# A decode-step gradient kernel: w1's gradient pass run backwards, its space lent slot by slot, a fifth wq chunk kept, and three zero-fill pieces moved

## The chip, the cores and the metric

The kernel runs on one core of one Trainium2 chip. The metric is the device time of one execution in microseconds; the median of several runs is compared. The core has a matrix engine (PE, whose weight loads are listed as PEld), a vector engine (DVE), an activation engine (ACT), a general engine (POOL), a queue engine that issues most DMAs (SP), and 16 DMA engines that move data between HBM and the on-chip memory.

## The reference

One token goes through two attention layers and two MLP layers that share their weights, and the result is the output and the gradients of all inputs but one.

```
x = x + A(layernorm(x)); x = x + B(layernorm(x))      # layer 0
x = x + A(layernorm(x)); x = x + B(layernorm(x))      # layer 1
A: q = n @ wq (1024 x 4096, 32 heads of 128); the last 4096 rows of a 32768-row cache, 4 kv heads;
   softmax(q k / sqrt(128)) v; @ wo (4096 x 1024)
B: h = n @ w1 + b1 (1024 x 3584); h * tanh(softplus(h)); @ w2 (3584 x 1024)
out = x, and by vjp(grad_out): gradients of x, k_cache, v_cache, wq, wo, w1, b1, w2
```

All is bf16. The gradients of the two caches are full size (32768 rows per head), and all rows but the last 4096 are zero. So a large part of the output is zeros, 56 pieces of 1 MB.

## The kernel before

The weights are too large to stay on the chip together, so they are read several times in chunks of 1 MB (128 partitions by 4096 bf16): wq and wo have eight chunks, w2 has seven, and w1 has eight parts of 896 KB, one for each t, which lie together in the tile W1 (W in the profile). The work stands in this order: forward through layers A, B, A, B; then the gradients backward, through B of layer 1 (dn_b1), A of layer 1 (attn_bwd with l = 1), B of layer 0 (the second reading of w2, then dn_b0), and A of layer 0 (attn_bwd with l = 0); then the outer products that make the weight gradients, and their stores. No planner reorders it: the order on each engine is the order in which the program is written, and waits between engines are put in from what each instruction reads and writes.

**The ring.** A class Ring holds eight slots of 1 MB. Loads are asked for with want, in a fixed order, and pump (L51 to L71) issues the next one on SP as soon as a slot is free. release frees the slot of a chunk when its last product has been written; keep renames a chunk in its slot, so that it needn't be loaded again; lend (L86) adds slots. Since SP issues DMAs in program order, whatever SP has to wait for holds up every load behind it.

**The chunks kept.** In attn_bwd of layer 1, the loop over wq's eight chunks (L915) transposes each chunk in place on PE in groups of eight blocks (L452), and DVE or ACT copies each group back (L305, L308). Chunks named in KEEP_Q2 (L268) stay in their slots, transposed, until attn_bwd of layer 0 uses them. The others are loaded again and transposed again.

**The second reading of w2** (L1102 to L1108). For each chunk c: mlp_out (L697), 32 products that finish the forward output; flush, which writes the products of the chunk before (L471); rows_chunk, two rows by DVE dot products (L429) and two by transposing; then the release of the chunk, which comes into effect after the next chunk's L697. Meanwhile the ring loads the rest of w2 and then wo (the key "o", 3).

**dn_b0** (L837). For each of the eight parts t of w1: a DVE dot over 512 columns and 24 products on PE. Behind parts 2 and 4 it writes row copies of vectors (rowize, take_back, rowize_f) into the space of w1's parts 0 and 1, ROWS and rf. They are small DMAs on SP: rowize first transposes on PE and copies on ACT (L978, L981), take_back reads back from DRAM what was put there. After dn_b0, lend gives the ring three more slots at once (L1118). They lie over w1's parts 4 to 7 (lent[0] over 4 and 5, lent[1] over 5 and 6, lent[2] over 6 and 7).

**attn_bwd of layer 0.** First the pass over wo's eight chunks with the hook do1(c) after each (rowize of GA at c = 0, and so on), then the scores' gradients with the hook dp1, then dq1, then the pass over wq with the hook dn1(t). The work units of the weight gradients (unit_dw, L1019, and units_kv, L1070) read ROWS and fill the rest of the time; they begin in dp1.

**The zero pieces.** zeros(n, after) (L256) issues n zero pieces from the tile zt on POOL's queue. With after, a tiny copy (L259) first waits until that value has been written; POOL works in order, so the pieces go out behind it. zt is set to zero in last_da (L761), which runs in the second attention's forward part, after the products with wq and before the scores. Until then zt holds a chunk of w2.

Of the kernel before, what the change touches and what calls it, by code (L numbers as in the profile page):

```python
# [23 lines left out]
TD = D // P  # L24
# [69 lines left out]
def kernel(  # L94
# [36 lines left out]
    def sb(shape, dtype, name):  # L131
        return keep.tile(shape, dtype, name=name)
# [3 lines left out]
    def tmp(shape, dtype, name):  # L136

        if name not in scratch:
            scratch[name] = keep.tile(shape, dtype, name=name)
        return scratch[name]  # L140
# [30 lines left out]
    def big():  # L171
        if wide:
            wide.append(wide.pop(0))
            return wide[-1][:, 0:512]
        b = bigs[big_n[0] % len(bigs)]
        big_n[0] += 1
        return b
# [22 lines left out]
    NA = sb([P, TD, 2], BF16, "NA")  # L200
    NB = sb([P, TD, 2], BF16, "NB")
    GA = sb([P, TD, 2], BF16, "GA")
    GB = sb([P, TD, 2], BF16, "GB")
    OC = sb([P, HQ, 2], BF16, "OC")
    DQC = sb([P, HQ, 2], BF16, "DQC")
    AC = sb([P, TF, 2], BF16, "AC")
# [13 lines left out]
    ring = Ring(nc, [ring_t[:, i, :] for i in range(8)])  # L220
# [9 lines left out]
    def want_q(k, ts=range(8)):  # L230
        for t in ts:
            ring.want(("q", k, t), wq_v[:, t, :], [P, J])

    def want_o(k, cs=range(8), homes=()):
        for c in cs:
            own = homes[c].rearrange("p (k d) -> p k d", k=4) if c < len(homes) else None
            ring.want(("o", k, c), wo_v[:, c], [P, 4, D], own, [("K", c)] if own is not None else [])
# [18 lines left out]
    def zeros(n, after=None):  # L256

        if after is not None and zjobs:
            nc.gpsimd.tensor_copy(pz[0:1, pz_n[0] % 16:pz_n[0] % 16 + 1], after[0:1, 0:1])  # L259
            pz_n[0] += 1  # L260
        for _ in range(n):
            if zjobs:
                dst = zjobs.pop()
                nc.gpsimd.dma_start(dst, zt[:])  # L264


    KEEP_Q = (5, 6, 7)
    KEEP_Q2 = (4, 5, 6, 7)  # L268
    EARLY_2 = (0, 1)
    MID_2 = (2, 3)  # L270
    W1S = W1[:].rearrange("p t f -> p (t f)")
# [17 lines left out]
    want_o(3)  # L289
    want_q(3, [t for t in range(8) if t not in KEEP_Q2])  # L290
    ring.pump()
# [35 lines left out]
    def bcast(col_of, n, dst=None):  # L327


        for i in range(n):  # L330
            k = i % 8
            nc.tensor.transpose(LB[i // 8][:, k * P:(k + 1) * P], col_of(i).to_broadcast([P, P]), ident_bf[:])
        if dst is not None:
            nc.vector.tensor_copy(dst, LB[0][:, 0:n * P])
# [87 lines left out]
    def rowdot(w, vecs, n, acc, fours=False):  # L422

        for i, vec in enumerate(vecs):
            out, a = junk[:, 0:n], w[:, i * n:(i + 1) * n]
            if fours:
                out, vec = (x.rearrange("a (k p) -> a k p", p=P) for x in (out, vec))
                a = a.rearrange("a (p k) -> a k p", k=4)
            nc.vector.tensor_tensor_reduce(out=out, in0=a, in1=vec, scale=1.0,  # L429
                                           scalar=acc if i else 0.0, op0=ALU.mult, op1=ALU.add, accum_out=acc)  # L430
        load["D"] += len(vecs) * (n * 1.1e-3 + 0.18)
# [33 lines left out]
    def mv_open():  # L465

        fresh[0] = True

    def mv(w, n, out, rhs_of, last):
        for i in range(n):  # L470
            nc.tensor.matmul(out, lhsT=w[:, i * P:(i + 1) * P], rhs=rhs_of(i), start=fresh[0], stop=last and i == n - 1,  # L471
                             skip_group_check=True)
            fresh[0] = False
# [3 lines left out]
    def turn_ahead(key, tts):  # L477

        for tt in tts:
            ahead[key, tt] = turn_pe(ring.get(key)[:, tt, :], TD)  # L480
# [152 lines left out]
    def conv(n, eng=None):  # L633
        for _ in range(n):
            conv_ev(conv_pe(1), eng)
# [92 lines left out]
    def da_dots(c, tts=range(4)):  # L728
        for tt in tts:
            r = 4 * c + tt  # L730
            rowdot(ring.get(("2", 0, c))[:, tt, :], [gbc], D, da1[:, r:r + 1])
# [21 lines left out]
    def last_da(k):  # L753

        for c in (5, 6):
            if k == 0:
                da_dots(c)
            else:
                ring.release(("2", 0, c))
        if k:  # L760
            nc.gpsimd.memset(zt[:], 0.0)  # L761

    def wo_hook1(c):
        if c == 0:
            zeros(7, OC[:, 0, 1:2])
        if c:
            conv(1)
# [13 lines left out]
    def take_back(name, base, off):  # L781
        r = DR[name][:].rearrange("(n l) p -> l n p", l=2)
        nc.sync.dma_start(ROWS[base:base + 2, off:off + r.shape[1] * P].rearrange("l (n p) -> l n p", p=P), r)
# [13 lines left out]
    dnp = sb([P, TD], FP32, "dnp")  # L797
# [18 lines left out]
    def rowize_f():  # L816

        b = big().bitcast(BF16)
        for l in range(2):
            for k in range(4):  # L820
                nc.tensor.transpose(b[0:7, (4 * l + k) * P:(4 * l + k + 1) * P],
                                    DHC[:, :, l].rearrange("p (c k) -> p k c", k=4)[:, k], ident_bf[:])
        nc.scalar.copy(rf.rearrange("c (l p k) -> c l p k", l=2, k=4), b[0:7].rearrange("c (l k p) -> c l p k", l=2, k=4))
        for l in range(2):
            nc.sync.dma_start(ROWS[64 + l:65 + l, NOFF:NOFF + F].rearrange("o (c j) -> o c j", j=512),
                              rf[:, 512 * l:512 * l + 512])
# [10 lines left out]
    def dn_b0(g):  # L837
        bcast(lambda c: DHC[:, c, 0:1], STAY)
        mv_open()
        for t in range(TD):  # L840
            rowdot(W1[:, t, 0:STAY * P], [LB[0][:, 0:512]], 512, dnp[:, t:t + 1], True)
            mv(W1[:, t, STAY * P:], TF - STAY, TP[:, t:t + 1], lambda i: DHC[:, STAY + i, 0:1], True)
            if t == 2:
                rowize(GB, TD, 96, 0)
                take_back("AC", 96, NOFF)
                take_back("NB", 64, 0)
                take_back("OC", 32, NOFF)
                take_back("NA", 0, 0)
            if t == 4:
                rowize_f()  # L850
        return ln_bwd(dnp, sB0["n32"], sB0["rstd"], g, "B0", lambda k: turn_ahead(("o", 3, 0), ((0,), (1, 2))[k]))

    DENSE = 2
# [100 lines left out]
    def dq3():  # L954
        zeros(3, DQC[:, 0, 1:2])

    g2 = attn_bwd(1, sA1, g3, ("o", 1), ("q", 2), KEEP_Q2,
                  dict(do=lambda c: conv(2 if 1 < c < 6 else 1), dp=dp3, dq=dq3, dn=lambda t: None),
# [4 lines left out]
    NOFF = 1024  # L963
# [7 lines left out]
    lent = [W1S[:, 16384 + i * SLOT:16384 + (i + 1) * SLOT] for i in range(3)]  # L971
# [3 lines left out]
    def rowize(cols, n, base, off):  # L975

        b = big().bitcast(BF16)
        nc.tensor.transpose(b[0:2 * n, 0:P], cols[:].rearrange("p n l -> p (n l)"), ident_bf[:])  # L978
        k = rt_n[0]
        rt_n[0] += 1  # L980
        nc.scalar.copy(rt[0:2 * n, k, :], b[0:2 * n, 0:P])  # L981
        for l in range(2):
            nc.sync.dma_start(ROWS[base + l:base + l + 1, off:off + n * P].rearrange("o (t p) -> o t p", p=P),
                              rt[l:2 * n:2, k, :])
# [40 lines left out]
    def units_rows(base, nblk, out):  # L1025

        for c in range(nblk // 4):
            s = stage_free.popleft()
            for tt in range(4):
                n = 0  # L1030
                while n < 2:
                    m = unit_dw(base, NOFF + (4 * c + tt) * P, 512 * n, s[:, tt * D + n * 512:(tt + 1) * D], 2 - n)
                    n += m
                    store(out.rearrange("(c p k) d -> p c (k d)", p=P, k=4)[:, c], s, 2 * tt + n - m, 2 * tt + n, 8,
                          c == nblk // 4 - 1)
                    yield
# [78 lines left out]
    nc.vector.tensor_copy(DHC[:, :, 0], dh0[:])  # L1115
    zeros(2, dh0)
    g1 = dn_b0(g2)
    ring.lend(lent)  # L1118
    nc.vector.tensor_copy(GA[:, :, 0], g1[:])

    x4 = sb([P, TD], BF16, "x4")
# [7 lines left out]
    do1_acc = tmp([P, HQ], FP32, "da")  # L1129

    def do1(c):
        if c == 0:
            rowize(GA, TD, 32, 0)
        if c == 3:
            todo[1].append(units_rows(32, HQ, out_5))
        if c == 5:
            store_rows(x4[:], TD, out_0[0, 0, :])
            store_f(db)
        if c == 5:
            zeros(2, do1_acc[:, 4 * c:4 * c + 1])  # L1140
# [10 lines left out]

    def dn1(t):
        if t in (3, 6, 7):
            zeros(2 if t == 3 else 1, dnp[:, t:t + 1])
        if t == 4:
            twins()
        if t == 5:
            todo[0].append(units_cols(0, 8, out_4))

    def units_a0(k):  # L1160
# [3 lines left out]
        work(4)  # L1164

    g0 = attn_bwd(0, sA0, g1, ("o", 3), ("q", 3), (), dict(do=do1, dp=dp1, dq=dq1, dn=dn1), units_a0)
    zeros(3, g0)
    g0b = sb([P, TD], BF16, "g0b")
    nc.vector.tensor_copy(g0b[:], g0[:])
    store_rows(g0b[:], TD, out_1[0, 0, :])  # L1170
# [46 lines left out]
```

## Time and profile before

| what | value |
|---|---|
| runs | 455.77 us median of 3 (455.38 to 458.13) |
| the profiled execution | 456.82 us, its span 455.0 us |
| busy in the span | PE 326.4, PE weight loads 262.1, DVE 258.8, ACT 210.6, POOL 38.8 us |
| moved by DMA | 181.48 MB, mean 399 GB/s |
| issued by SP or ACT / by POOL | 121.84 MB / 58.72 MB |

The page cuts the span into 40 slices and gives each engine's busy share in tenths, the share of the DMA engines, and what they moved. Other views give the same for any stretch, list instructions in order of time with the idle time before each and what ended it, or add up who waited for whom. A time in a view is microseconds from the start of the span.

### The profile page before, as it was taken

To read this page: it belongs to the slowest core of one execution; us is meant where nothing else is said; L and a number is where in the kernel's file an instruction comes from. 1 tells how busy PE (TensorE), PEld (TensorE's weight loads), DVE (VectorE), ACT (ScalarE), POOL (GpSimd) and SP (SyncE) were. 2 spreads that over 40 slices of the span, in tenths; PEclk is the share of its full clock that TensorE was granted. 3 is DMA by queue.
4 is the path that set the end of the run, shared out by engine and by line. 5 is a ranking of instruction groups with operands and counts; after the bars stand their busy time and mean duration, and the time that the engine had idled before them with its cause. 6 is when DMAs were issued, how large, how long until landed. Compare 5 with 4: busy or idle time off the path is not lost. (4 is left out here: it accounts for less than half of the span.)

```text
span 455.0 us, 14050 instructions
## 1 busy us (share of the span) xinstructions
PE 326.4 (72%) x6289; PEld 262.1 (58%) x6289; DVE 258.8 (57%) x508; ACT 210.6 (46%) x245; POOL 38.8 (9%) x86
## 2 busy tenths in 40 slices
PE   3836543456599788898797988798977898889500
PEld 3735443456598778797797877796861222235300
DVE  4504747277450075477366847486377999888600
ACT  2501001011055276687066452283349999999500
POOL 1000000002032221200210101012221000000000
PEclk9955555555555588999589655697675555555555
DMA  8999999989989999999999899999999999999996
GB/s 336 424 418 418 421 416 419 419 321 421 421 349 403 401 407 412 410 393 418 420 419 421 341 402 333 361 371 416 421 420 420 417 421 423 423 419 419 404 408 248
DMA packets 28091, 181.48 MB, mean 399 GB/s; under 512 B 3675, under 2 KB 3703, under 8 KB 9463
## 3 DMA queue, kind: packets, MB, share of 16 engines
q1 hardware_dynamic: 19874, 121.84, 66.1%
q0 software_dynamic: 8064, 58.72, 31.6%
q8 instruction: 49, 0.80, 0.7%
q14 instruction: 12, 0.09, 0.0%
q10 hardware_dynamic: 92, 0.02, 0.0%
HBM read 81.84 MB, written 98.62 MB: 397 GB/s over the span
## 5 line engine op out<-in xcount | busy, mean ns | idle before, releaser
L308 ACT COPY ring<-BIG 128x1024 bf16<-128x1024 bf16 x51 | 50.5, 1015 | 44.0 <-PE BIG L452 37.6
L1019 PE MATMUL wide<-W 2*128 2x512 bf16 x228 | 52.1, 598 | 9.3 <-ACT W L308 2.0
L452 PE MATMUL BIG<-ident_bf,ring 128*128 128x128 bf16 x664 | 55.5, 238 | 1.4 <-ACT ring L308 0.4
L452 PEld LDWEIGHTS <-ring 128*128 128x128 bf16 x768 | 53.2, 109 | 2.4 <-issue 1.7
L429 DVE CUSTOM_DVE_ANT_0 junk<-ring,SC 128x1024 bf16<-128x1024 bf16 x32 | 38.9, 1215 | 6.7 <-DMA ring<-in_B_w_dram 6.2
L1019 PEld LDWEIGHTS <-W 2*128 2x128 bf16 x240 | 12.6, 102 | 44.3 <-issue 43.2
L471 PEld LDWEIGHTS <-ring 128*128 128x128 bf16 x864 | 29.9, 97 | 10.5 <-issue 6.8
L305 DVE CAST ring<-wide 128x1024 bf16<-128x1024 f32 (+1 forms) x29 | 33.7, 1200 | 3.2 <-PE wide L1019 1.5
L308 ACT COPY KT<-BIG 128x1024 bf16<-128x1024 bf16 x22 | 21.9, 1011 | 27.5 <-PE BIG L625 26.0
L308 ACT CAST ring<-wide 128x1024 bf16<-128x1024 f32 (+1 forms) x35 | 32.9, 1018 | 1.3 <-PE wide L1070 0.5
L305 DVE COPY ring<-BIG 128x1024 bf16<-128x1024 bf16 x32 | 21.8, 689 | 16.6 <-PE BIG L452 12.7
L264 POOL DMA_DIRECT2D out_dram<-zt x56 | 29.7, 534 | 15.0 <-DMA out_dram<-zt 14.2
L429 DVE CUSTOM_DVE_ANT_0 junk<-ring,DSX 128x1024 bf16<-128x1024 bf16 x24 | 29.4, 1224 | 0.8
L645 PE MATMUL MV<-NB,W 128*128 128x1 bf16 x448 | 16.5, 172 | 15.5 <-DMA W<-in_B_w_dram 12.7
L645 PEld LDWEIGHTS <-W 128*128 128x128 bf16 x448 | 15.8, 118 | 16.3 <-DMA W<-in_B_w_dram 13.4
L452 PE MATMUL BIG<-ident_bf,W 128*128 128x128 bf16 x288 | 23.3, 227 | 2.4 <-issue 2.4
L514 PE MATMUL MV<-NA,ring 128*128 128x1 bf16 x512 | 15.2, 165 | 13.1 <-DMA ring<-in_A_wq_dram 11.8
L308 ACT COPY W<-BIG 128x1024 bf16<-128x1024 bf16 x21 | 20.6, 1015 | 7.9 <-PE BIG L452 7.4
L514 PEld LDWEIGHTS <-ring 128*128 128x128 bf16 x512 | 14.6, 103 | 13.9 <-DMA ring<-in_A_wq_dram 12.4
L305 DVE CAST VS<-wide 128x1024 bf16<-128x1024 f32 (+1 forms) x17 | 19.7, 1187 | 3.6 <-PE wide L1019 3.0
L1070 PE MATMUL wide<-W 32*128 32x256 bf16 x128 | 20.9, 402 | 0.9 <-ACT ring L308 0.6
L308 ACT CAST KT<-wide 128x1024 bf16<-128x1024 f32 x20 | 20.4, 1032 | 1.8 <-PE wide L1019 0.9
(258 smaller groups left out, 551.5 us busy)
## 6 DMA issues: line engine op xcount, KB each, us to landing
out_dram<-zt POOLq DMA_DIRECT2D x56, 1024.0 KB, 15.1
ring<-in_A_wq_dram SPq DMA_DIRECT2D x24, 1024.0 KB
ring<-in_A_wo_dram SPq DMA_DIRECT2D x14, 1024.0 KB
ring<-in_B_w_dram SPq DMA_DIRECT2D x13, 1024.0 KB
W<-in_A_wo_dram SPq DMA_DIRECT2D x10, 1024.0 KB
W<-in_B_w_dram SPq DMA_DIRECT2D x8, 896.0 KB
out_dram<-ring SPq DMA_DIRECT2D x7, 1024.0 KB
out_dram<-ring SPq DMA_DIRECT2D x13, 512.0 KB
```

The source lines that it names most:

```text
L264: nc.gpsimd.dma_start(dst, zt[:])
L305: nc.vector.tensor_copy(dst, src)
L308: nc.scalar.copy(dst, src)
L429: nc.vector.tensor_tensor_reduce(out=out, in0=a, in1=vec, scale=1.0, scalar=acc if i else 0.0, op0=ALU.mult, op1=ALU.add, accum_out=acc)
L452: nc.tensor.transpose(b[:, i * P:(i + 1) * P], block(w, i) if block else w[:, i * P:(i + 1) * P], ident_bf[:])
L471: nc.tensor.matmul(out, lhsT=w[:, i * P:(i + 1) * P], rhs=rhs_of(i), start=fresh[0], stop=last and i == n - 1, skip_group_check=True)
L514: nc.tensor.matmul(q_ps[:, h:h + 1], lhsT=ch[:, h * P:(h + 1) * P], rhs=NA[:, t, l:l + 1], start=(k == 0 and h == 0), stop=(k == TD - 1), ...
L645: nc.tensor.matmul(h_ps[:, fb:fb + 1], lhsT=f_block(W1[:, t], fb), rhs=NB[:, t, l:l + 1], start=(t == 0 and fb == 0), stop=(t == TD - 1), ...
L1019: nc.tensor.matmul(b[:, 512 * i:512 * i + 512], lhsT=R[at:at + 2, lo:lo + P], rhs=R[at:at + 2, ro + 512 * i:ro + 512 * i + 512], start=Tru ...
L1070: nc.tensor.matmul(b[:, k * 256:(k + 1) * 256], lhsT=RT[32 * g:32 * g + 32, a, tp, :], rhs=YS[32 * g:32 * g + 32, :], start=True, stop=Tru ...
```

## The change

Five edits:

- KEEP_Q2 gets chunk 3 of wq: five chunks stay transposed in their slots between the two backward attention layers, and chunks 0 to 2 are loaded again.
- dn_b0 runs over w1's parts from 7 down to 0. After part 6 it lends the slot over parts 6 and 7, after part 5 the one over 5 and 6, after part 4 the one over 4 and 5.
- The row copies that stood in dn_b0 stand in do1: rowize of GB at c = 0, the four take_backs at c = 1, rowize_f at c = 2.
- One zero piece is issued right after zt is set to zero, and one in do1 at c = 1, behind the first column of da (do1_acc).
- One zero piece less is issued in dn1 at t = 3, and one less at the end (two, not three). The total stays 56.

```
-    KEEP_Q2 = (4, 5, 6, 7)
+    KEEP_Q2 = (3, 4, 5, 6, 7)
...
         if k:
             nc.gpsimd.memset(zt[:], 0.0)
+            zeros(1)
...
     def dn_b0(g):
         bcast(lambda c: DHC[:, c, 0:1], STAY)
         mv_open()
-        for t in range(TD):
+        for t in reversed(range(TD)):
             rowdot(W1[:, t, 0:STAY * P], [LB[0][:, 0:512]], 512, dnp[:, t:t + 1], True)
             mv(W1[:, t, STAY * P:], TF - STAY, TP[:, t:t + 1], lambda i: DHC[:, STAY + i, 0:1], True)
-            if t == 2:
-                rowize(GB, TD, 96, 0)
-                take_back("AC", 96, NOFF)
-                take_back("NB", 64, 0)
-                take_back("OC", 32, NOFF)
-                take_back("NA", 0, 0)
-            if t == 4:
-                rowize_f()
+            if 4 <= t < 7:
+                ring.lend([lent[t - 4]])
...
     g1 = dn_b0(g2)
-    ring.lend(lent)
...
     def do1(c):
         if c == 0:
             rowize(GA, TD, 32, 0)
+            rowize(GB, TD, 96, 0)
+        if c == 1:
+            take_back("AC", 96, NOFF)
+            take_back("NB", 64, 0)
+            take_back("OC", 32, NOFF)
+            take_back("NA", 0, 0)
+            zeros(1, do1_acc[:, 0:1])
+        if c == 2:
+            rowize_f()
...
     def dn1(t):
         if t in (3, 6, 7):
-            zeros(2 if t == 3 else 1, dnp[:, t:t + 1])
+            zeros(1, dnp[:, t:t + 1])
...
-    zeros(3, g0)
+    zeros(2, g0)
```

## The prediction

> **What bounds the kernel now.** I read the page's 40 slices first, then stretches of the span, then the matmuls of one pass in order of time, then the waits of SP's DMA queue.
>
> ```profile
> DMA  8999999989989999999999899999999999999996
> GB/s 336 424 418 418 421 416 419 419 321 421 421 349 403 401 407 412 410 393 418 420 419 421 341 402 333 361 371 416 421 420 420 417 421 423 423 419 419 404 408 248
> HBM read 81.84 MB, written 98.62 MB: 397 GB/s over the span
> ```
>
> The DMA engines are busy in nearly every slice, at about 419 GB/s where nothing holds them up. So the end is bytes over rate plus the stretches in which the rate falls. One piece or chunk is 1.049 MB, 2.5 us at that rate. The falls lie in three places; the columns are length, then busy time of PE, its weight loads, DVE, ACT and POOL, then granted clock, DMA share, GB/s:
>
> ```profile
> 115.00:132.50 17.50, 13.77 (x338) 12.73 (x341) 7.82 (x18) 5.57 (x8) 0.21 (x1) 0.50 1.01 419
> 132.50:135.00 2.50, 2.09 (x82) 2.09 (x82) 1.49 (x4) 0.90 (x1) 1.93 (x4) 0.50 0.34 141
> 250.00:252.50 2.50, 2.15 (x38) 1.81 (x36) 1.17 (x7) 0.00 (x0) 0.71 (x2) 1.00 0.97 410
> 252.50:255.00 2.50, 2.07 (x67) 1.92 (x65) 2.32 (x3) 1.30 (x2) 0.00 (x0) 0.93 0.96 380
> 255.00:257.50 2.50, 2.50 (x57) 2.50 (x54) 2.43 (x5) 1.11 (x2) 0.00 (x0) 0.50 0.65 200
> 257.50:260.00 2.50, 2.33 (x59) 2.25 (x58) 2.43 (x5) 1.54 (x2) 0.70 (x2) 0.50 0.83 328
> 277.50:280.00 2.50, 1.82 (x56) 1.83 (x57) 1.69 (x7) 0.00 (x0) 1.25 (x3) 0.50 1.00 318
> 280.00:282.50 2.50, 2.50 (x79) 2.36 (x77) 2.36 (x9) 0.25 (x1) 0.00 (x0) 0.50 0.92 223
> 282.50:287.50 5.00, 2.66 (x77) 2.39 (x75) 2.06 (x6) 1.00 (x1) 0.00 (x0) 0.50 0.99 412
> 287.50:290.00 2.50, 2.50 (x31) 2.50 (x29) 1.28 (x10) 0.19 (x1) 0.00 (x0) 0.50 0.83 270
> 310.00:345.00 35.00, 28.40 (x622) 23.38 (x622) 18.52 (x43) 12.68 (x20) 8.99 (x21) 0.68 1.01 420
> 345.00:430.00 85.00, 72.84 (x388) 26.27 (x384) 76.96 (x69) 78.75 (x87) 0.00 (x0) 0.50 1.01 418
> 430.00:452.00 22.00, 0.00 (x0) 0.00 (x0) 0.00 (x0) 0.00 (x0) 0.00 (x0) 0.50 0.95 380
> ```
>
> From 310 on the DMA is never short of work, and for the last 22 us it works alone: compute is done by 430. A faster engine there buys nothing. I therefore count in DMA time: bytes taken away, plus lost time added, minus lost time filled.
>
> **Part by part.**
>
> *The fifth kept chunk.* One read of wq goes: 2.5 us of DMA, **-2.5**. With it go 24 transposes (L452, 0.47 us for eight at full clock) and three copies (L308, 1.0 us) in the last wq pass, at 320 to 340. I price these at nothing: the DMA runs at 420 there and compute has 22 us of slack at the end.
>
> *The price of keeping it* is a ring slot from the second layer's wq pass on: three slots are left for w2's second reading, not four. Its loads go out at 234.4, 236.5, 239.1 and 240.6, and the fifth at 256.23, when the first chunk is released. The fourth now goes at 256.23. So 2.5 us of transfers leave 250 to 260, where (rows above) 0.05+0.23+1.31+0.54 = 2.1 us are lost already. About 0.7 us of it is filled by zeros that the next part pushes back: **+1.8** (from 0 to +2.5).
>
> *A zero piece at the second scores.* It stands behind the memset of zt alone, which ends at 114.4, so it goes to a DMA that is full (419) and pushes wo's chunks back by 2.5 us, the last from 134.6 to 137.1. The wo pass needs that one at 144.9: no wait. The hole at 132.5 (141 of 419: 1.66 us, and 0.2 behind it) is filled: **-1.8** (0 to -2.5). POOL's copy of QC waits 0.5 us more; nothing near reads it.
>
> *The w2 pass with three slots.* PE in order of time, start and length, L697 being the first product of each chunk:
>
> ```profile
> 257.68 1.04 PE L697 MATMUL MV<-AC,ring 128*128 128x1 bf16 x32
> 260.99 1.04 PE L697 MATMUL MV<-AC,ring 128*128 128x1 bf16 x32
> 264.30 1.04 PE L697 MATMUL MV<-AC,ring 128*128 128x1 bf16 x32
> 268.87 1.02 PE L697 MATMUL MV<-AC,ring 128*128 128x1 bf16 x32 [1.05 <-DMA ring<-in_B_w_dram]
> 272.65 1.01 PE L697 MATMUL MV<-AC,ring 128*128 128x1 bf16 x32 [0.60 <-DMA ring<-in_B_w_dram]
> ```
>
> A chunk takes 3.31 us; its slot is freed 1.87 us into the next one (257.68, load at 259.55). With four slots a load has 256.23 to 264.30, 8.07 us; with three, 4.76. The load of 259.55 took 9.3 us behind others; on an idle DMA (issued 256.23) half of the 16 engines were done in 4.5 us. Step by step, 2.5 us per transfer: chunk 3 from 258.2 lands at 261, in time. Chunk 4 queues behind it and the zero piece issued at 257.93: 266.2 against 264.3. Chunk 5, asked for at 262.9, lands by 269 and starts at 269.8 when PE is free. Chunk 6, asked for at 268.1, queues behind a zero piece that chunk 4 released late: 274.7 against 272.65. The pass ends 2 us later, and the DMA idles some 1.3 us more in it: **+1.3** (0 to +4).
>
> *w1 backwards, slots lent one by one.* Now, the stretch of dn_b0 loses 0.60+1.17+0.08+0.89 = 2.7 us: one chunk is in flight, and the three lent slots are asked for only at 287.6. A step is 0.73 us of DVE (L429) and 0.70 of PE, so from a start at 280.6 the lent loads go at about 282.4, 283.1 and 283.8. Beside them lie three zero pieces: the one added in wo's pass waits on a column last written before dh0, so POOL issues it right behind the two of dh0. That is seven transfers, full until about 298.5: **-2.4** (-2.7 to -1).
>
> *The row copies moved into wo's pass.* Taken from dn_b0: nine transposes (0.27 and 1.06 us of PE). Added to wo's pass: the same, and ACT copies of 0.26 and 1.00 us beside 1.0 us evictions: about as much later there as sooner here, nothing in the sum. SP's queue is dearer. In the built order SP's DMAs take eight counters in turn, and each waits until the DMA that had its counter has landed. The trace shows such a wait:
>
> ```profile
> SPq L825 <- DMA ring<-in_A_wo_dram: 1.3, 1, 1.3
> ```
>
> Now four row copies, four take_backs and then the load of wo's chunk 6 stand in a line behind the lent loads, and in that order two take_backs wait for lent chunks to land (299 for the last). Each small DMA holds SP 0.4 to 0.7 us, and chunk 6's counter waits for a row copy, issued at 295 and landing 5.5 us later as now. So chunk 6 goes at about 300.4, not 296.2, and the DMA is empty from 298.7 to 301.9, where 0.2 us are lost already: **+3.0** (0 to +4). Chunk 6 lands at 305.5, needed at 304.7: 0.5 us of wait, in the bounds.
>
> *The zero pieces that went* (one at dn's chunk 3, one at the end): 13 are left from 311 on, not 15. The last now lands at 361.3 and the first result store goes at 345.8, so two fewer (5 us) leave no hole: 0 (to +1.5).
>
> Sum: -2.5+1.8-1.8+1.3-2.4+3.0 = **-0.6 us**. Check from the other side: wo's pass ends 2 us later (312.3), 2.1 MB less are then to be issued (-5.0), and of the seven transfers asked for since 301.9 some 3.0 MB wait in the queues, against 2.2 now (+1.9): -1.1. The profiled execution took 456.82 (span 455.0); it becomes 456.2. The median of the runs is 1.05 lower, 455.77; it becomes **455.2**. About 1% (4.6 us) is what a measurement of this kernel can tell from no change.
>
> The Trainium skill (DMA: Bandwidth & Descriptors, Where 436 GB/s comes from) has HBM transfers bound at about 358 GB/s. The trace disagrees, at 419. By that figure the chunk would be worth 2.9 us and the sum -1.0.
>
> **The rivals.**
>
> *The loads keep up.* Chunk 4 lands in time, as landings half-way (4.5 us) would have it, and the small copies land before chunk 6 is due: +0.3 in place of +1.3 and +0.5 in place of +3.0, -4.1 in all: 451.7. For it: the DMA is emptier in front of this pass. Against it: two waits on these loads with four slots.
>
> *Three slots starve the w2 pass (slower).* If a load takes the 9.3 us of 259.55 each time, chunk 3 starts at 265.5, 4 at 268.9, 5 at 276.7, 6 at 280.0: 7.4 us late, not 2. That is 5.4 more than in the check, of which the smaller backlog gives back about 1: 455.2+4.5 = 459.7. It decides once loads take over 6.5 us. Against it: those 9.3 us were spent behind three other transfers; with three slots fewer stand in line.
>
> *wo's pass at half clock.* The granted clock is 0.50 from 255 and 1.00 only from 292.5, just as wo's pass begins; if it waits on chunks it may stay at 0.50. Eight transposes then take 0.93 us (L452 at 256.02 to 257.9), not 0.47, and a chunk with three such groups 3.65 of PE, where now DVE's 2.14 pace it: eight of them 12 us, of which the shorter backlog gives back 5: 462. The Trainium skill (TensorE: Matmul & The Clock Gate, What's actually happening) drops the clock after an idle window of 3.4 us; here it fell at 254.6 with PE 83% busy in the 2.5 us up to 255, so the trace does not agree with it. The waits that I expect are under 1 us.
>
> That a chunk less is read and 56 zero pieces stay is in the built order, so that it doesn't do what it says gets no chance.
>
> **How the numbers follow.** Forecast 0.53 (453 to 458 by itself), loads keep up 0.20, starved 0.20, half clock 0.04, other 0.03. The range drops half of the outer cases: 451.3 to 460.6. Faster by over 1% (below 451.2) needs the second case and a little more: 0.10. Slower by over 1% (above 460.3): a bad half of the third and the fourth: 0.18. Within: 0.72.
>
> **What would show it.** The stretch 132.5 to 135 near 400 GB/s; 252 to 258 emptier than now; L697's waits on DMA at some 3 us, not 1.65, and its last chunk at 274.7; 280 to 297 near 415; SP's take_backs waiting on DMAs of wo, and a hole at 298 to 302; POOL's DOC copy (311.5 now) at 313 to 314. Wrong if L697 hardly waits (then 452), if it waits over 6 us (then 460), or if the DMA falls under 400 after 312, where I count nothing.

## The result, and the profile after

The changed kernel takes 463.35 us (median of six, 461.15 to 465.03), the kernel before 457.73 beside it: a ratio of **1.0119** (1.0085 to 1.0153). Measured once more beside others it came to 1.0131 (1.0094 to 1.0168). So it is 5.4 to 6 us slower; 455.2 was predicted, with a range up to 460.6. The profiled execution took 462.76 (span 461.0; 455.0 before).

The 40 slices of the changed kernel's profile: the busy share of the DMA engines in tenths, what they moved, and the total.

```profile
DMA  8999999989999999999999889959899999999998
GB/s 336 422 420 420 419 419 417 422 316 423 391 424 414 410 412 412 411 395 422 418 425 371 332 292 345 424 192 390 360 398 373 412 412 417 418 421 415 408 406 326
HBM read 80.79 MB, written 98.62 MB: 389 GB/s over the span
```

One chunk less is read (80.79 MB, 81.84 before). Before, the DMA was full from 310 on; now a slice near 300 has less than half its rate and some behind it are below 400. Stretches of the changed kernel, columns as in the prediction (length, busy time of PE, its weight loads, DVE, ACT, POOL, then granted clock, DMA share, GB/s):

```profile
117.50:120.00 2.50, 2.15 (x81) 2.08 (x79) 0.69 (x1) 0.00 (x0) 0.00 (x0) 0.50 1.00 305
125.00:145.00 20.00, 19.01 (x444) 18.49 (x445) 6.12 (x14) 10.51 (x12) 4.29 (x8) 0.50 1.01 418
250.00:280.00 30.00, 23.19 (x481) 21.28 (x481) 17.11 (x33) 13.58 (x14) 2.13 (x6) 0.58 0.86 316
280.00:300.00 20.00, 15.31 (x309) 14.85 (x310) 10.96 (x38) 3.45 (x6) 1.90 (x5) 0.53 0.99 385
300.00:320.00 20.00, 11.21 (x272) 10.66 (x268) 9.16 (x15) 11.01 (x13) 1.23 (x3) 0.90 0.73 271
312.50:317.50 5.00, 0.00 (x0) 0.00 (x0) 0.16 (x1) 0.03 (x1) 0.00 (x0) 0.86 0.98 337
320.00:360.00 40.00, 33.16 (x663) 26.27 (x664) 22.74 (x49) 15.92 (x23) 7.97 (x19) 0.59 0.95 383
436.00:461.00 25.00, 3.10 (x20) 1.49 (x16) 4.36 (x4) 3.27 (x4) 0.00 (x0) 0.50 0.93 369
```

Time lost in a stretch is its length times (1 - rate / 420), 420 GB/s being the rate of a full stretch. The kernel before moves 373, 368, 352, 398 and 420 GB/s in the five long stretches from 125 to 360, and 336 in its last 25 us. That gives, in us of DMA time:

| stretch | what is there | lost before | lost after | changed | predicted |
|---|---|---|---|---|---|
| 125 to 145 | hole at the second scores | 2.2 | 0.1 | -2.1 | -1.8 |
| 250 to 280 | w2's pass with three slots | 3.7 | 7.4 | +3.7 | +1.8 +1.3 |
| 280 to 300 | dn_b0, w1 backwards | 3.2 | 1.7 | -1.5 | -2.4 |
| 300 to 320 | wo's pass, the row copies | 1.0 | 7.1 | **+6.1** | +3.0 |
| 320 to 360 | wq's pass, zero pieces | 0.0 | 3.5 | **+3.5** | 0 |
| last 25 us | the last stores alone | 5.0 | 3.0 | -2.0 | 0 |
| | one chunk less | | | -2.5 | -2.5 |

With 0.7 us more in the row 117.5 to 120 (416 GB/s before) this is +5.9; the spans differ by 6.0. Up to 300 us the stretches follow the prediction, each within 1 us; from 300 on they do not. At 312.5 to 317.5 PE has no instruction at all. What it waits for, in PE's and POOL's order of time:

```profile
309.95 0.62 PE L452 MATMUL BIG<-ident_bf,ring 128*128 128x128 bf16 x8 [0.64 <-DMA ring<-in_A_wo_dram]
320.00 1.03 PE L452 MATMUL BIG<-ident_bf,ring 128*128 128x128 bf16 x8 [7.96 <-DMA ring<-in_A_wo_dram]
325.62 0.21 POOL L872 COPY DOC<-DOC 128x32 bf16<-128x32 bf16 x1 [16.14 <-DVE DOC L871]
```

The first wait is for wo's chunk 6 (0.5 us of wait was in the prediction), the second for chunk 7. POOL's copy of DOC, behind which four zero pieces are issued, comes at 325.62 instead of 311.54. By about 325 the DMA has moved the last wq load, and from 325 to 327 its rate is 148 and 90 GB/s, until those pieces start: that is the first hole behind 320. SP's queue of the changed kernel, in order of time, tells why chunk 7 is late (start, length, line, what is copied, how many):

```profile
295.61 2.87 SPq L978 DMA_DIRECT2D W<-W  x4
298.57 0.38 SPq L784 DMA_DIRECT2D W<-dr_AC  x1
299.01 0.29 SPq L784 DMA_DIRECT2D W<-dr_NB  x1
303.00 0.23 SPq L784 DMA_DIRECT2D W<-dr_OC  x1
303.27 0.32 SPq L784 DMA_DIRECT2D W<-dr_NA  x1
303.70 0.36 SPq L71 DMA_DIRECT2D ring<-in_A_wo_dram  x1
304.16 1.56 SPq L826 DMA_DIRECT2D W<-W  x2
312.97 0.37 SPq L71 DMA_DIRECT2D ring<-in_A_wo_dram  x1
313.45 0.84 SPq L71 DMA_DIRECT2D ring<-in_A_wq_dram  x1
314.46 2.48 SPq L71 DMA_DIRECT2D W<-in_A_wq_dram  x2
```

and the waits of that queue from 290 to 330 (what was waited for: us in total, times, longest):

```profile
SPq L71 <- DMA out_dram<-W: 7.2, 1, 7.2
SPq L784 <- DMA W<-in_A_wo_dram: 3.7, 1, 3.7
```

Two things hold this queue up, one behind the other. The row copies and take_backs come first: one of them waits 3.7 us for the last lent chunk to land (303.0), and the first load into a released slot, chunk 6's, goes at 303.70; 300.4 was predicted. The kernel before has its first such load at 296.2, but there it is chunk 7's: with four wq chunks kept, seven chunks of wo find a slot before any chunk of wo is released, with five only six. So two loads of wo stand behind this line, not one. Then chunk 7's load waits 7.2 us for a store to DRAM out of W. That is x4, 2 KB, issued by **ACT** in do1 at c = 5 (309.05, landed 312.9). In the built order SP's and ACT's DMAs share the eight counters (a DMA adds to its counter as it lands), and with the row copies standing among the loads x4's store comes just eight places ahead of chunk 7's load. The trace records the counter of every DMA: the eight are numbered 100, 102 to 106, 109 and 110, and both x4's store and chunk 7's load have 106. In this order the store stands between the first and the second take_back, although the source calls it four chunks later. It is issued when chunk 5 is through, so chunk 7 could not be asked for before that, and all three wq loads stand behind it. In the kernel before another DMA took that counter, a row copy of DQC. SP waited for the store there too, behind the last load, where it held up nothing; the trace of before shows it among the waits of SP's queue:

```profile
SPq L983 <- DMA out_dram<-W: 6.4, 1, 6.4
```

The first products of w2's chunks (L697), for the step that was right:

```profile
261.31 1.01 PE L697 MATMUL MV<-AC,ring 128*128 128x1 bf16 x32 [0.61 <-DMA ring<-in_B_w_dram]
266.66 1.01 PE L697 MATMUL MV<-AC,ring 128*128 128x1 bf16 x32 [2.19 <-DMA ring<-in_B_w_dram]
270.23 1.01 PE L697 MATMUL MV<-AC,ring 128*128 128x1 bf16 x32 [0.39 <-DMA ring<-in_B_w_dram]
275.06 1.01 PE L697 MATMUL MV<-AC,ring 128*128 128x1 bf16 x32 [1.66 <-DMA ring<-in_B_w_dram]
```

They wait 4.9 us in all (some 3 were predicted), and the last chunk starts at 275.06 (274.7 predicted); the starved case had 280.

### The profile page after: what moved, and what is told of

Read it like the earlier page. It is cut to its first block, busy times and chain, and to the rows that moved or that the text cites. A ratio compares the mean times of both kernels' runs of the same rounds, so it can differ in the third digit from the quotient of the medians.

```text
span 461.0 us, 13994 instructions
## 1 busy us (share of the span) xinstructions
PE 325.9 (71%) x6265; PEld 261.9 (57%) x6265; DVE 259.1 (56%) x507; ACT 208.4 (45%) x243; POOL 39.0 (8%) x87
## 3 DMA queue, kind: packets, MB, share of 16 engines
HBM read 80.79 MB, written 98.62 MB: 389 GB/s over the span
## 5 line engine op out<-in xcount | busy, mean ns | idle before, releaser
L308 ACT COPY ring<-BIG 128x1024 bf16<-128x1024 bf16 x49 | 48.7, 1014 | 61.8 <-PE BIG L452 55.3
L452 PE MATMUL BIG<-ident_bf,ring 128*128 128x128 bf16 x624 | 55.6, 248 | 11.2 <-DMA ring<-in_A_wo_dram 8.6
L452 PEld LDWEIGHTS <-ring 128*128 128x128 bf16 x712 | 52.5, 114 | 12.5 <-DMA ring<-in_A_wo_dram 8.9
L1014 PE MATMUL wide<-W 2*128 2x512 bf16 x228 | 52.1, 598 | 9.3 <-ACT W L308 1.9
L1014 PEld LDWEIGHTS <-W 2*128 2x128 bf16 x240 | 12.6, 102 | 44.3 <-issue 43.2
L471 PEld LDWEIGHTS <-ring 128*128 128x128 bf16 x832 | 29.2, 99 | 7.2 <-issue 4.0
L305 DVE COPY ring<-BIG 128x1024 bf16<-128x1024 bf16 x29 | 19.8, 690 | 19.3 <-PE BIG L452 12.4
L452 PE MATMUL BIG<-ident_bf,W 128*128 128x128 bf16 x304 | 23.3, 219 | 1.9 <-issue 1.9
L514 PEld LDWEIGHTS <-ring 128*128 128x128 bf16 x512 | 14.6, 103 | 14.0 <-DMA ring<-in_A_wq_dram 12.6
```

The source lines that it names most:

```text
L305: nc.vector.tensor_copy(dst, src)
L308: nc.scalar.copy(dst, src)
L452: nc.tensor.transpose(b[:, i * P:(i + 1) * P], block(w, i) if block else w[:, i * P:(i + 1) * P], ident_bf[:])
L514: nc.tensor.matmul(q_ps[:, h:h + 1], lhsT=ch[:, h * P:(h + 1) * P], rhs=NA[:, t, l:l + 1], start=(k == 0 and h == 0), stop=(k == TD - 1), ...
L1014: nc.tensor.matmul(b[:, 512 * i:512 * i + 512], lhsT=R[at:at + 2, lo:lo + P], rhs=R[at:at + 2, ro + 512 * i:ro + 512 * i + 512], start=Tru ...
```

## The experiments

Three theories stood at first: (1) x4's counter holds chunk 7; (2) the slot given to the fifth chunk starves w2's pass; (3) the zero pieces that went from the end leave the late holes. All ratios are to the kernel before, measured beside each; 0.001 is 0.46 us.

**Both of ACT's stores late.** x4's and db's store go from c = 5 to dq1.

```
     def dq1():
         rowize(DQC, HQ, 0, NOFF)
+        store_rows(x4[:], TD, out_0[0, 0, :])
+        store_f(db)
```

> The changed kernel, with the two small result stores that ACT issues at do1's c = 5 (x4's and db's) issued in dq1 instead. Theory 1 (wo's chunk 7 load is held by the counter of x4's store): the load goes at about 305 instead of 312.97, PE's wait at L452 on wo falls from 8.6 us to under 1, the DMA is above 350 GB/s from 307 on, and the 5 to 8 us go: 455 to 458, a ratio to the kernel before of 0.995 to 1.002. Theory 2 (the loss is the slot that the fifth chunk takes, w2's pass): nothing there changes, 461 to 464, ratio 1.008 to 1.015. Theory 3 (too few zero pieces late): the holes of 322 to 330 and 345 to 355 stay, 460 to 463.

Measured: 1.0257 (1.0223 to 1.0291), slower still. Chunk 7's load did go early, at 304.77, and PE's waits for wo fell to 1.6 us. But x4's staging row is the one that the row copies of DQC use, so ACT had to wait for those to land, and PE and the zero pieces waited for ACT:

```profile
335.19 0.25 ACT L324 COPY W<-BIG 8x128 bf16<-8x128 bf16 x1 [6.90 <-DMA W<-W]
```

The wait was cured and a new one made, so this run can't give the price of the first. Its profiled execution, 462.4 us, was well below its others (466 to 471), which the profile doesn't explain.

**db's store alone late.** This shifts the order of counters by one place and nothing else near it.

```
         if c == 5:
             store_rows(x4[:], TD, out_0[0, 0, :])
-            store_f(db)
```

> The changed kernel, with only db's store moved to dq1; x4's store stays at c = 5. One DMA less stands between x4's store and wo's chunk 7 load, so by the built order the load takes the counter of the first take_back, and the first wq load takes that of x4's store. Theory 1: chunk 7's load goes at about 305, PE waits under 1.5 us for it, while wq's first load now goes at 312 to 313; between the changed kernel and the one with both stores moved, 457 to 461. If the place of ACT's stores in time mattered and not the counter, both loads would go as in the changed kernel (313) or both early.

Measured: 1.0080 (1.0057 to 1.0103). SP's queue in that run:

```profile
304.68 0.36 SPq L71 DMA_DIRECT2D ring<-in_A_wo_dram  x1
305.14 1.67 SPq L826 DMA_DIRECT2D W<-W  x2
306.92 0.38 SPq L71 DMA_DIRECT2D ring<-in_A_wo_dram  x1
315.09 0.33 SPq L71 DMA_DIRECT2D ring<-in_A_wq_dram  x1
```

Chunk 7 now goes at 306.92 and the first wq load, which has taken its place in the order, is the one that is held, to 315.09, when x4's store (issued 309.18, landed 315.02) is through. Whoever takes the counter waits, as expected; the trace gives chunk 7's load counter 105 here, and x4's store and the first wq load both 106. The holes from 320 to 360 shrink to 0.8 us (412 GB/s) with the same zero pieces, so theory 3 falls: the pieces were not too few, they were let go too late, behind PE's wait.

**The fifth chunk alone**, in the kernel before.

```
-    KEEP_Q2 = (4, 5, 6, 7)
+    KEEP_Q2 = (3, 4, 5, 6, 7)
```

> The kernel before, with the fifth wq chunk kept and nothing else changed. By the sum of the prediction: -2.5 for the read, +1.8 for the emptier 250 to 260 (+2.5 without the zero pieces pushed there), +1.3 for w2's pass: 0.6 to 1.3 us slower, ratio 1.001 to 1.003. Theory 2 (this edit is the whole loss): 4 to 6 us slower, ratio 1.009 to 1.013. If it gained the read alone: 0.995.

Measured: 1.0090 (1.0064 to 1.0115), 4 us slower: theory 2 has its part too. The stretch 250 to 280 runs at 281 GB/s (9.9 us lost), 300 to 320 at 367 (2.5).

**Four chunks kept, all else changed.**

> The changed kernel with four wq chunks kept again, all else as in the changed kernel. Theory 2: most of the loss goes, 456 to 458. Theory 1: by the built order wo's chunk 6 is then lent a slot sooner and the DMA that takes the counter of x4's store is the first of four wq loads; PE no longer waits 8 us in wo's pass, but the wq loads go at 311 to 313 instead of 298 to 303, and one more chunk is read: 459 to 464, ratio 1.004 to 1.014.

Measured: 1.0026 (1.0001 to 1.0052), less than the counter theory expected, more than theory 2 did. 300 to 320 still loses 7.2 us (268 GB/s): the DMA with the counter of x4's store (109 here) is the first wq load, and it goes at 313.17. But no PE wait for chunk 7 follows, and 320 to 360 loses only 0.4.

**Both stores in dp1**, behind all loads and ahead of DQC's row copies.

> The changed kernel, with both small stores of ACT issued in dp1, behind all loads of wo and wq, so that no load takes their counters, and ahead of the row copies of DQC, so that ACT doesn't wait for those as it did with the stores in dq1 (6.9 us at L324). Counter theory: chunk 7's load at about 305, wq's loads from 305.5 to 308, no hole after 320; 0.5 to 2 us less than with db's store alone moved (1.0080): ratio 1.004 to 1.007. What is left then is the fifth chunk's slot. If the prediction's price for that slot (0.6 us in all) were right, it would come to 0.998 to 1.001.

Measured: 1.0086 (1.0065 to 1.0108). Chunk 7 at 305.86, wq's loads from 306.34 to 307.73, 411 GB/s from 320 to 360. So the counter's share of the loss is 1.5 to 2 us by the ratios, each good to 1 to 1.5 us; the version comes out above the 1.004 to 1.007 expected. 300 to 320 still loses 5.1 (312 GB/s): chunk 6 went at 303.73, behind the row copies.

**w1 backwards alone**: slots lent one by one, row copies moved, four kept, zero pieces as before; and the same with both stores in dp1.

> The kernel before, with w1 run backwards, the slots lent one by one and the row copies moved into wo's pass; four chunks kept and the zero pieces as before. By the prediction's terms -2.4 and +3.0: 0.6 us slower, 1.001. By the counter theory the first of four wq loads takes the counter of x4's store and goes at 311 or later, not at 298: about 6 us lost at 300 to 310 against 1.1, less 1.6 gained before: 3 to 4.5 us slower, 1.007 to 1.010.

> The kernel before with w1 backwards, slots lent one by one and row copies moved (1.0134 alone), and ACT's two stores moved to dp1 besides, so that no wq load takes the counter of x4's store. If that counter is most of the loss at 300 to 310: wq's first load at 303 to 305 instead of 312, 3 us less lost there, ratio 1.005 to 1.009. If SP's line of small copies is most of it: 1.011 to 1.014, with the loads after chunk 6 still late.

Measured: 1.0134 (1.0113 to 1.0156) and 1.0082 (1.0053 to 1.0111). In the first the wq loads start at 311.99 (7.5 us of wait for the store), in the second at 303.38; 300 to 320 loses 7.2 and 3.2 us. With four chunks kept the counter costs 2.4 us, and the rest of this edit 3.8.

**One zero piece at the second scores**, one less at the end.

> The kernel before, with one zero piece issued right behind the memset of zt, and one less at the end. The hole at 132.5 is filled and nothing else changes: by the prediction -1.8 us, ratio 0.996. If the filled hole were given back (the piece that goes at the end opens a hole there): 1.000.

Measured: 0.9976 (0.9955 to 0.9998), -1.1 us. 125 to 145 runs at 418 GB/s instead of 373, -2.1; but 117.5 to 120 falls from 416 to 301, +0.7. The dip is in all thirteen profiles with this piece (301 to 341) and in none of the six without it (413 to 423).

**Row copies later.** Four chunks kept; rowize of GB at c = 3, the take_backs at c = 4, rowize_f at c = 5; both stores in dp1.

> The changed kernel with four chunks kept, the row copies of GB, the take_backs and rowize_f two to three chunks later in wo's pass (c = 3, 4, 5), behind wo's last load and the first wq loads in SP's queue, and ACT's two stores in dp1. If SP's line and the counter are what cost the four-chunk version its gain, 300 to 310 loses about 1 to 2 us as in the kernel before (not 6), the gains of the zero piece (2.2) and of dn_b0 (1.6 to 1.9) stay: 452.5 to 455.5, ratio 0.989 to 0.996. If the loss at 300 to 310 has another cause: 457 to 459, as with four chunks kept alone (1.0026).

Measured: 1.0036 (1.0008 to 1.0065), and the profile says why it isn't less. The stretches first, then a wait of PE and one of SP's queue from 290 to 330 (total us, times, longest):

```profile
280.00:300.00 20.00, 18.01 (x398) 17.45 (x396) 13.99 (x39) 8.45 (x11) 0.00 (x0) 0.71 1.01 422
300.00:320.00 20.00, 13.14 (x327) 11.61 (x324) 10.09 (x21) 7.54 (x9) 3.55 (x8) 0.80 1.01 420
```

```profile
PE BIG L1014 <- DMA W<-W: 9.4, 1, 9.4
```

```profile
SPq L826 <- DMA out_dram<-W: 7.8, 1, 7.8
```

With the loads first in SP's queue the DMA is full from 280 to 320. But the four work units of dp1 (L1014) read those rows, the last row copy (L826) waits 7.8 us for x4's store, whose counter (100 here) it has, PE waits 9.4 for it, and 8 us are lost from 320 to 360. The row copies too have a time by which they must have landed.

**Work units late too.** As the last, without the four units in dp1 and with the stores in dn1 at t = 6; with four chunks kept, then with five.

```
     def dp1():
-        work(4)
...
     def dn1(t):
+        if t == 6:
+            store_rows(x4[:], TD, out_0[0, 0, :])
+            store_f(db)
```

> As the run with late row copies and four chunks kept, but the four work units of dp1 are left to the later places (they waited 9.4 us for the row copies there), and ACT's two stores stand in dn1 at t = 6. With the loads ahead of the row copies in SP's queue and nothing in dp1 that needs them, no hole from 280 to 360: losses of some 12 us by 320 as in that run (before: 18) and none after; 449 to 453, ratio 0.980 to 0.990. If the work units' wait was only a symptom (the zeros late for another reason), the holes from 320 to 350 stay: 457 to 460.

> The same with five chunks kept, as in the changed kernel. By the mean of the profiles so far, w2's pass with three slots loses 3.3 us more in 250 to 280 than with four, and the read that goes is 2.5: 0 to 2 us slower than the four-chunk version beside it. If the fifth chunk costs 4 us as alone in the kernel before: 4 us slower than it.

Measured: 0.9942 (0.9911 to 0.9972) and 0.9991 (0.9963 to 1.0020). In both the late holes are gone (419 GB/s from 320 to 360). The first is faster than the kernel before, but by 2.6 us, not by the 5 to 9 expected. Its last stretches, and those of the changed kernel, show where some of that stayed:

```profile
440.00:445.00 5.00, 0.00 (x0) 0.00 (x0) 0.00 (x0) 0.00 (x0) 0.00 (x0) 0.50 1.02 409
445.00:452.50 7.50, 0.00 (x0) 0.00 (x0) 0.00 (x0) 0.00 (x0) 0.00 (x0) 0.50 0.22 87
```

```profile
450.00:455.00 5.00, 0.00 (x0) 0.00 (x0) 0.00 (x0) 0.00 (x0) 0.00 (x0) 0.50 1.02 408
455.00:461.00 6.00, 0.00 (x0) 0.00 (x0) 0.00 (x0) 0.00 (x0) 0.00 (x0) 0.50 0.62 248
```

In the four-chunk version most of the 16 DMA engines are done soon after 446 and a few run on to 451.6: of the last store's 16 landings the median is at 446.5 and the last at 451.6. In the changed kernel they are 1.0 us apart, in the kernel before 3.8. A reading of this, which no run tests: some engines fall behind, and catch up in holes where the others have nothing to do; without holes they carry the lag to the end.

**The changed kernel again**, for a second profile.

> The changed kernel once more, beside the others on one chip, for a second profile: 1.009 to 1.015 again; chunk 7's load again held by x4's store to 311 to 314, PE's longest wait on wo 6 to 9 us, and 3 to 5 us of DMA lost from 320 to 360. If the holes after 320 were chance of one execution: under 1 us there.

Measured: 1.0131 (1.0094 to 1.0168). Chunk 7's load at 311.75, the longest wait 6.4 us, 4.0 us lost from 320 to 360: the holes are not chance.

**What the late versions owe to the units alone.** The changed kernel with units and stores late but its row copies at c = 0, 1, 2; the kernel before with units and stores late; and the best version with w1 forwards again.

> The changed kernel with its row copies where the change puts them (c = 0, 1, 2), but the four work units of dp1 left out and ACT's two stores in dn1 at t = 6, as in the five-chunk version at 0.9991; it differs from that version in the place of the row copies alone. Theory of SP's line (small copies ahead of wo's chunks 6 and 7 in SP's queue hold their loads): chunk 6 at 303 to 304, 3.5 to 5 us lost from 300 to 320, ratio 1.006 to 1.009. Rival (the gain came from the units taken out of dp1, or from the stores): 0.998 to 1.002.

> The kernel before with the four units of dp1 left out and ACT's two stores in dn1 at t = 6. Theory of SP's line: there is no hole there to fill, 0.998 to 1.002. Rival (units and stores are a gain by themselves): 0.992 to 0.996, and the best version's gain is theirs.

> The best version so far (four chunks kept, zero pieces moved, units and stores late, 0.9942) with w1 forwards again, the three slots lent together and the row copies in dn_b0, as in the kernel before. The prediction gave backwards and lending one by one 2.4 us; the profiles show 1.1 to 1.6 less lost from 280 to 300: 0.997 to 1.000. If backwards is worth nothing once its row copies are out of the way: 0.994.

Measured: 1.0051 (1.0028 to 1.0074), 0.9993 (0.9973 to 1.0013) and **0.9914** (0.9887 to 0.9942). The first differs from the five-chunk version (0.9991) in the place of the row copies only. The 300 to 320 rows of the two, row copies early and late:

```profile
300.00:320.00 20.00, 13.07 (x280) 12.67 (x277) 9.11 (x19) 9.21 (x10) 1.96 (x5) 0.72 0.85 336
```

```profile
300.00:320.00 20.00, 17.32 (x458) 16.42 (x455) 12.97 (x26) 10.56 (x12) 3.54 (x8) 0.86 0.99 394
```

4.0 against 1.2 us lost, and 2.7 us by the ratios: that is SP's line. The second shows that units and stores gain nothing by themselves. The third was a surprise: w1 forwards is not slower than backwards, and by its median, 453.87 us, it is the fastest kernel of all.

**The zero pieces alone**, all three edits, and only the one in wo's pass (with one less in dn1), in the kernel before.

> The kernel before with the three zero-piece edits and nothing else (one at the second scores, one in do1 at c = 1, one less in dn1 and one less at the end). The version with these and with units and stores late came to 0.9914; units and stores late alone to 0.9993. If the zero pieces are the whole gain: 0.990 to 0.994. If they gain only beside late units and stores: 0.996 to 1.000.

> The kernel before with one zero piece moved from dn1's t = 3 to do1's c = 1, where POOL issues it right behind the two of dh0. The prediction counted this piece within the -2.4 of dn_b0. If it fills the hole of 280 to 290 (2.3 us lost there) and nothing gives it back: 0.994 to 0.997. If the loads behind it come so much later: 0.998 to 1.001.

Measured: 0.9946 (0.9928 to 0.9965) and 0.9951 (0.9928 to 0.9975): -2.5 and -2.2 us. The profile of the second doesn't show where its gain comes from: 280 to 300 runs at 356 GB/s there (352 before), and the profiled execution was the slowest of its twelve. In the profile of the first this stretch runs at 389.

So there is a chain of kernels from the one before to the changed one, one step at a time:

| kernel | ratio | step, us | predicted |
|---|---|---|---|
| before | 1 | | |
| + the zero pieces | 0.9946 | -2.5 | -1.8, and a part of -2.4 |
| + units and stores late | 0.9914 | -1.5 | not in the change |
| + w1 backwards, slots lent singly, row copies late in wo's pass | 0.9942 | +1.3 | the rest of -2.4 |
| + the fifth chunk | 0.9991 | +2.2 | -2.5 +1.8 +1.3 |
| + row copies to c = 0, 1, 2 | 1.0051 | +2.7 | +3.0 |
| + units and stores in dp1 | 1.0086 | +1.6 | not in the change |
| + stores at c = 5: the changed kernel | 1.0119, 1.0131 | +1.5, +2.1 | none |

Each ratio is good to some 0.002 to 0.004 either way (1 to 2 us), so a single step of 1.5 us is not certain; the sum is. One pair checks two steps: w1 backwards with early row copies, on top of the kernel before and without the counter's wait, cost 3.8 us above, and 1.3 + 2.7 is 4.0 here.

## Why the prediction was wrong, step by step

**The sum.** Predicted were -0.6 us, measured 5.4 to 6. By the chain the miss has three parts, each known to some 2 us only: the zero pieces and w1 backwards together brought 1.2 us, not 4.2; the fifth chunk cost 2.2, not 0.6; and the wait for ACT's store, which had no term, cost 1.5 to 2.1.

**The step whose mechanism failed is "the row copies moved into wo's pass", +3.0.** It was half right: the small copies stand in SP's queue ahead of chunk 6, and a take_back waits for a lent chunk. That line alone measures +2.7, about its price, though the last lent chunk lands at 303.0, not 299, and chunk 6 goes 3.3 us later than predicted. What was missing is the second wait behind it. The step followed the counters of SP's own copies to chunk 6 and stopped there. Chunk 7's load waits for a counter that ACT's x4 store holds, 7.2 us (+1.5 to +2.1 as a price). With both, 300 to 320 lost 6.1 us more than before in the first profile and 4.2 in the second (309 GB/s).

**"The zero pieces that went: 0" failed as its consequence.** It rested on the DMA being full from 311 on. It was full because zero pieces were let go by POOL's copy of DOC at 311.54; PE's wait moved that copy to 325.62. The prediction had it at 313 to 314. 3.5 and 4.0 us were lost from 320 to 360 in the two profiles; in the first, the last 25 us lost 2.0 less than before. The sign "the DMA falls under 400 after 312" was met.

**The fifth chunk: mis-sized.** Its three terms gave +0.6. Measured are +2.2 on top of the version without late holes, and 4 us alone in the kernel before or between four and five chunks in the changed kernel. The price in w2's pass agrees in the mean: over eleven profiles with four chunks kept, 250 to 280 runs at 349 GB/s (5.1 us lost, from 3.7 to 6.7), over eight with five at 305 (8.2): +3.1, as predicted. The stretches behind it were priced at nothing, and there the pairs lost more too: 1.5 us in 300 to 320 with the fifth chunk alone, 3.1 in 320 to 360 in the changed kernel against four chunks kept. One read less is a gain only if something else is ready in its place. How much of the 2 to 4 us is that, and how much the scatter of 250 to 280, isn't told apart.

**w1 backwards, -2.4: mis-sized, and given to the wrong edit.** The term took backwards, lending one by one and one zero piece together. By the ratios this zero piece gains 2.2 us by itself (0.9951), with w1 forwards, and backwards with late row copies adds to the zero pieces nothing that shows (+1.3, with an uncertainty of about 2). The profiles show a smaller gain in the stretch itself: 280 to 300 loses 1.5 to 2.0 us in nine of the ten profiles with backwards and the zero piece (none in the tenth), 2.5 to 3.2 in the four with neither. With only one of the two the profiles scatter from 1.5 to 3.6, so which of them fills the hole isn't told apart there.

**The second scores, -1.8: right in kind.** The hole went (-2.1), and a dip at 117.5 that was not foreseen took back 0.7; -1.1 by the ratio.

**w2's pass, +1.8 and +1.3: right in its mechanism**, with 275.06 for 274.7; in the first profile the stretch lost 3.7 us more, not 3.1, and PE waited 4.9, not 3. So the rival "starved" fell, and with it "the loads keep up". "wo's pass at half clock" fell as a cause: the granted clock was 0.90 over 300 to 320, and PE was waiting there. It fell to 0.50 behind the waits: eight transposes (L452) took 1.03 us for chunk 7, not 0.61, and in the second profile for chunk 6 too.

The prediction weighed 358 GB/s from the Trainium skill (DMA: Bandwidth & Descriptors, Where 436 GB/s comes from) against 419 in the trace. Full slices of the changed kernel again have 419 to 425, so the trace's figure stands. Another section of that page of the Trainium skill (Anatomy of one DMA, on GpSimd's path) says that semaphore waits are made by the issuing sequencer before the DMA is handed over, never by the DMA engines. The trace agrees, here for SP: it stands still for 7.2 us at one load, and the three loads behind it in the queue go only when that one has gone.

## What to carry to other kernels

When small DMAs are moved, list every DMA of all engines that share completion counters, in the order as built and not as the source has it, and look at who held the counter of each big load behind them, not only the first: a 2 KB store of another engine can hold a megabyte. Follow a late load to what it lets go (here POOL's copy and the zero pieces) before calling a full DMA queue a cover. And price the cheapest filler of a hole alone (one zero piece moved: 2.2 us) before counting on a restructuring for the same hole.

## What the runs showed of the hardware

- A 2 KB store issued by ACT took 3.9 us to land beside two zero pieces of 1 MB (309.05 to 312.9), 5.8 with db's store late (309.18 to 315.02), and 3.7 to 6.0 us over all nineteen profiles. In the six profiles in which a DMA on SP waited last for this store's counter, it went within 0.1 us of the landing.
- The 16 DMA engines do not end together: 1.0 us between the median and the last landing of the last store in the changed kernel, 3.8 in the kernel before, 5.1 in the four-chunk version with late units, which loses least from 125 to 360 (6.8 us). So a hole filled in the middle need not be gained in full at the end.
- With a zero piece among the first wo loads, 117.5 to 120 ran at 305 GB/s (301 to 341 in twelve other profiles; 413 to 423 in the six without it) while the DMA engines were busy all the time (share 1.00). The cause stays open.
- The stretch 250 to 280 varied from 326 to 368 GB/s between kernels whose code is the same up to there, but for the zero piece at 115 in six of the eleven. The prediction's base, the profile of before, was the best of them.
